# A weight product partly in float32r, and the set-up of one batch put in another order (one core)

## The chip, the core and the metric

The kernel runs on one core of a Trainium2 chip. The metric is the time of one execution on the device in microseconds (us); smaller is better. Inside the core several engines work side by side, each through its own list of instructions in a fixed order: TensorE (PE in the profile, with its weight loads shown apart as PEld), VectorE (DVE), ScalarE (ACT), GpSimd (POOL, hardly used here) and SyncE (SP, which issues DMA transfers). They wait for each other through semaphores.

## The reference

```
# attention of 512 tokens x with 32 state rows, both ways, per batch (8) and head (8), D = 64
a  = softmax(scale * x @ state^T);   xread = a  @ state
a2 = softmax(scale * state @ x^T);   sread = a2 @ x
X  = concat(xread, sread) as rows of 512        # 8 * (512 + 32) = 4352 rows
# bilinear feed-forward layer
h   = ((X @ w1) * (X @ w2)) @ w3                # w1, w2: 512 x 1024, w3: 1024 x 1024
out = h @ w_out                                 # w_out: 1024 x 512
```

The weights w1, w2, w3 and w_out come as 64-bit floats and are read as their bits; x and state come as 32-bit floats.

## The kernel before, in words

**Weights.** Each weight arrives in pieces of 128 x 1024 64-bit words (tile `raw`) and is turned into 32-bit floats by `to_f32`, in two steps: two ScalarE passes (lines 120 and 130) and then two VectorE passes, a shift (line 134) and an integer addition (line 138, a custom instruction). A caller takes the two steps one by one with `go`. There are eight pieces of w_out with half of w3, four more pieces of w3, and eight of w1 and w2 (`convert_half(n)`, n = 0 to 7). Piece n of w1 and w2 goes into `places[n]`, which is column quarter n // 2 of matrix n % 2 (0 is w1, 1 is w2) in the tile `w_sb`.

**wo = w3 @ w_out.** The reference's two last products are replaced by one with wo = w3 @ w_out, which is computed first, in eight tiles i = 0 to 7. Tile i is the sum over eight chunks k of a 128 x 128 block of w3 with `w_out[k]`, 512 columns wide, in one PSUM bank. Tiles 0 to 3 grow together while the weights arrive (`w34_first`), tiles 4 to 7 come one after the other (`w34(i)`, line 635). A float32 product stands as two records in the trace. For the chunks 4 and 6 (`SPLIT`) the first four tiles do it otherwise: each operand is split into a high part, rounded to float32r, and a low part, the remainder (`split`: a cast on ScalarE, line 99, and a subtraction on VectorE, line 100), and three float32r products (high x high, high x low, low x high; line 612) take the place of one float32 product.

`finish(i)` splits tile i of wo into its two parts, by a cast and a subtraction that read the bank. The pool `ps_o` has two banks which the tiles take in turn, so `w34(6)` needs `finish(4)` done, `w34(7)` needs `finish(5)`, and the first two accumulators of the token output (`early_stage2`) need `finish(6)` and `finish(7)`. While wo is computed, `w_out[0:8]` lies in `places[4:8]`, two chunks to a place: a conversion into place 4 + m has to wait until the last tile's product with chunks 2m and 2m + 1 has been done.

**One batch.** The scores of a batch (line 151, with x) are turned, reduced and exponentiated on VectorE and ScalarE; this gives the attention weights `at`, split into high and low. State times w1 and w2 gives the tiles `sw`, also split: for batch 0 the column half 0 is made in quarters by `sets(quarter)` (line 151 again, two products of eight pieces each, in a pool `ps_2` of three buffers), half 1 later by `sw_steps(0)[2:]`, which makes one `sw` tile from w1 (places 4 and 6) and one from w2 (places 5 and 7). `stage1(0, ft)` for ft = 0 to 7 then multiplies `sw` with `at` (line 344, 12 float32r products 128 x 512 in a block), multiplies the two results elementwise (a ScalarE copy, line 325, and a VectorE product, line 326) and splits the result into `g`. `early_stage2(quarter)` multiplies `g` with wo (line 358). So the order around the first blocks of batch 0 is: stage1 ft 0, ft 1, ft 2, the two products of half 1, `early_stage2(0)`, stage1 ft 3, and so on. After batch 0 the others follow in another form, which the change leaves alone.

**What sets the order.** TensorE and SyncE follow the order of the program. ScalarE and VectorE follow it too up to `order.close()` (line 701); behind it a scheduler sets their order by priority, and `tc.issue_after(x)` keeps the instructions in its block behind x. In either case the order is fixed when the program is built.

## Time and profile before

| | |
|---|---|
| three runs before | 488.54, 488.63, 489.65 us; median 488.63 |
| the profiled execution | 487.95 us, of which the span from the first to the last instruction is 486.2 |
| granted TensorE clock | 1.0 of full speed, over the whole span |
| busy share of the span | TensorE 99%, weight loads 76%, VectorE 81%, ScalarE 49% |
| set-up of wo and of batch 0 (up to the first stage-1 block) | 0 to 66 us |

A row of the timeline gives the start in us, the busy time in us, the engine, the line of the program, the operation, output<-input, the shape, the number of records and, in brackets, the idle time of the engine before it with what ended that. The chain of waits gives start, duration and the piece of work that ended last at that point. The changed program has other line numbers: one less between the old lines 35 and 291, and six more at the old line 635.

### The profile page before, as it was taken

What the parts mean: (1) busy time and instruction counts of PE and PEld (TensorE: products, weight loads), DVE (VectorE), ACT (ScalarE), POOL (GpSimd) and SP (SyncE); (2) the same over time, 40 slices, a digit from 0 to 9 for tenths busy, and PEclk for the clock granted to TensorE, in tenths of its full rate; (3) what the DMA queues carried; (4) which work ended last, traced back from release to release, by engine and by line L of the source; (5) the groups of instructions that cost most, each with busy time, mean ns of one, the idle gap of its engine ahead of it and who ended that gap; (6) DMA issues with size and microseconds to landing.
All of it is one profiled execution on the core that took longest, in us unless ns stands there. A gap on an engine that the chain in (4) does not pass through costs nothing.

```text
span 486.2 us, 8627 instructions
## 1 busy us (share of the span) xinstructions
PE 479.5 (99%) x3398; PEld 370.2 (76%) x3398; DVE 393.4 (81%) x580; ACT 237.6 (49%) x368; POOL 0.2 (0%) x4
## 2 busy tenths in 40 slices
PE   8999999999999999999999999999999999999996
PEld 5554467768788878887797779777977797899885
DVE  5778999798899589959985998599859985678870
ACT  4876984453547045605560555055515642353640
POOL 0000000000000000000000000000000000000000
PEclk9999999999999999999999999999999999999999
DMA  8996971163014404130413042304230223001101
GB/s 345 367 399 222 388 278 26 19 216 89 14 38 173 106 4 182 38 93 4 182 41 92 5 181 45 87 5 181 47 84 6 89 47 85 5 2 45 45 1 43
DMA packets 56361, 52.49 MB, mean 108 GB/s; under 512 B 42752, under 2 KB 50944, under 8 KB 51712
## 3 DMA queue, kind: packets, MB, share of 16 engines
q1 hardware_dynamic: 47488, 43.27, 26.8%
q10 hardware_dynamic: 8832, 8.65, 5.2%
q8 instruction: 27, 0.44, 0.4%
q14 instruction: 14, 0.11, 0.1%
HBM read 38.27 MB, written 8.91 MB: 97 GB/s over the span
## 4 chain that ended last, share of the span: by engine, by line
PE 93%; DVE 4%; ACT 1%; DMA 1%; issue 0%; DVEq 0%; ACTq 0%
PE ps L344 36%; PE ps_o L460 11%; PE ps L472 8%; PE ps L151 8%; PE ps_o L358 7%; PE ps_o L465 6%; PE ps L477 4%; PE ps L756 3%; PE ps_o L615 2%; PE ps L615 2%; PE ps_o L635 2%; PE ps L758 2%; PE ps_o L276 1%; DVE w_sb L138 1%; DMA raw<-in_w_k_dram 1%; PE ps L612 1%
## 5 line engine op out<-in xcount | busy, mean ns | idle before, releaser
L344 PE MATMUL ps<-at_lo,sw_hi 128*128 128x512 f32 x256 | 101.1, 395 | 0.0
L344 PE MATMUL ps<-at_hi,sw_hi 128*128 128x512 f32 x256 | 99.7, 389 | 0.0
L344 PE MATMUL ps<-at_hi,sw_lo 128*128 128x512 f32 x256 | 99.7, 389 | 0.0
L549 ACT COPY tmp<-ps 128x512 f32<-128x512 f32 x56 | 32.8, 585 | 121.5 <-PE ps L344 119.3
L344 PEld LDWEIGHTS ps<-at_lo,sw_hi 128*128 128x128 f32 x256 | 48.1, 188 | 15.9 <-DVE g_lo L100 4.2
L344 PEld LDWEIGHTS ps<-at_hi,sw_lo 128*128 128x128 f32 x256 | 48.1, 188 | 10.3
L344 PEld LDWEIGHTS ps<-at_hi,sw_hi 128*128 128x128 f32 x256 | 48.1, 188 | 9.5 <-issue 0.2
L488 DVE TENSOR_TENSOR tmp<-tmp,ps 128x512 f32<-128x512 f32 x42 | 28.9, 688 | 19.0 <-PE ps L477 18.1
L429 DVE TENSOR_TENSOR g_x<-tmp,ps 128x512 f32<-128x512 f32 x28 | 19.0, 679 | 26.4 <-ACT tmp L549 26.3
L100 DVE TENSOR_TENSOR sw_lo<-ps,sw_hi 128x1024 fp32r<-128x1024 f32 (+1 forms) x34 | 38.2, 1149 | 1.3 <-ACT sw_hi L99 1.3
L99 ACT CAST g_hi<-raw 128x512 fp32r<-128x512 f32 x42 | 24.6, 619 | 29.1 <-DVE raw L429 21.6
L151 PE MATMUL ps<-w_sb,st 64*32 64x512 f32 (+1 forms) x544 | 31.6, 570 | 0.4 <-DVE sw_lo L100 0.4
L99 ACT CAST sw_hi<-ps 128x1024 fp32r<-128x1024 f32 (+1 forms) x34 | 31.1, 969 | 1.8 <-PE ps L151 1.7
L460 PEld LDWEIGHTS ps_o<-t,g_hi 128*128 128x128 f32 x224 | 27.8, 191 | 5.0 <-issue 5.0
L99 ACT CAST g_hi<-g_x 128x512 fp32r<-128x512 f32 x42 | 25.6, 625 | 10.3 <-DVE g_x L429 5.3
L460 PE MATMUL ps_o<-t,g_hi 128*128 128x256 f32 x224 | 29.7, 286 | 0.0
L100 DVE TENSOR_TENSOR g_lo<-raw,g_hi 128x512 fp32r<-128x512 f32 x42 | 28.0, 681 | 1.6 <-PE ps_o L465 1.6
L460 PE MATMUL ps_o<-wo,g_hi 128*128 128x256 f32 x224 | 29.1, 283 | 0.0
L460 PEld LDWEIGHTS ps_o<-wo,g_hi 128*128 128x128 f32 x224 | 28.3, 192 | 0.5
L100 DVE TENSOR_TENSOR g_lo<-g_x,g_hi 128x512 fp32r<-128x512 f32 x42 | 27.2, 684 | 1.8 <-PE ps_o L465 1.8
L472 PE MATMUL ps<-t,g_hi 128*128 128x512 f32 x112 | 28.0, 392 | 0.0
L472 PEld LDWEIGHTS ps<-t,g_hi 128*128 128x128 f32 x112 | 20.2, 189 | 3.6
(125 smaller groups left out, 802.6 us busy)
## 6 DMA issues: line engine op xcount, KB each, us to landing
raw<-in_w_k_dram SPq DMA_DIRECT2D x8, 1024.0 KB, 6.0
x_d<-in_x_d_dram SPq DMA_DIRECT2D x8, 1024.0 KB, 7.4
raw<-in_w_dram SPq DMA_DIRECT2D x8, 1024.0 KB, 6.6
x_s<-in_x_s_dram SPq DMA_DIRECT2D x8, 1024.0 KB, 5.1
out_dram<-tmp ACTq DMA_DIRECT2D x56, 128.0 KB, 1.8
raw<-in_w3t_dram SPq DMA_DIRECT2D x4, 1024.0 KB, 7.0
e<-work SPq DMA_DIRECT2D x112, 32.0 KB, 2.0
sread<-turned SPq DMA_DIRECT2D x128, 4.0 KB, 1.7
```

Source lines behind the costliest of these rows:

```text
L99: nc.scalar.copy(out=hi, in_=src),
L100: nc.vector.tensor_tensor(out=lo, in0=src, in1=hi.bitcast(F32), op=ALU.subtract),
L151: nc.tensor.matmul(ps[j * NS:(j + 1) * NS, q], sts[b][rows, j], moving(rows, j), start=True, stop=True)
L344: nc.tensor.matmul(ps[:, i], w[:, kt, c:c + P], a[:, kt], start=(k == 0), stop=(k == 3 * KT - 1))
L358: nc.tensor.matmul(ps[:, :DO], g, wo[w][:, ft, :], start=(ft == 0 and k == 0), stop=(ft == FT - 1 and k == 2))
L460: nc.tensor.matmul(ps[:, tt * HO:(tt + 1) * HO], g, w(part, k), start=(fresh and k == 0 and tt == 0 and part == "lo"), stop=False, skip_gr ...
L465: nc.tensor.matmul(ps[:, tt * HO:(tt + 1) * HO], g, w("hi", k), start=False, stop=(k == QF - 1), skip_group_check=True)
L472: nc.tensor.matmul(ps[:, tt].rearrange("p (n d) -> p n d", n=2), g, w(k), start=(k == 0), stop=False, skip_group_check=True,)
L477: nc.tensor.matmul(ps[:, tt, :HO], g, w(k)[:, 0], start=False, stop=(k == QF - 1), skip_group_check=True)
L488: sum2 = lambda out, x, y: nc.vector.tensor_tensor(out=out, in0=x, in1=y, op=ALU.add)
L549: copied = nc.scalar.copy(out=a_sb, in_=ps[:, 0])
L615: nc.tensor.matmul(w34_ps[i][:, :DO], chunks[k][:, DO + i * P:DO + (i + 1) * P], w_out[k], start=(k == 0), stop=(k == FT - 1),)
```

## The change

There are three parts.

1. Tile 6 of wo does its chunks 4 and 6 with float32r products, as tiles 0 to 3 do. The parts of w_out that were split for those are kept and used again; the two blocks of w3 are split by a new function, `split_columns(6)`, one cast and one subtraction of 128 x 256, which stand right behind the conversion of w3's tile 6.
2. Tile 7 of wo does all its eight products before `sets(1)`, not five before and three behind. In between stand the conversions of w1's and w2's third column quarter (`convert_half(4)` and `(5)`, first steps behind the second and the fourth product; second steps ahead of and behind `sets(1)`), which a scheduler placed before.
3. `finish(6)` and `finish(7)` move out of the hand-written order, behind `convert_half(6)` and `(7)`, and behind the splits of `sets(1)`.

```
-LAST = 5
@@ sw_quarter
-        split(*(t[:, :, c * NQ:(c + 1) * NQ] for t in tiles[half, i]), ps)
+        last_split[:] = split(*(t[:, :, c * NQ:(c + 1) * NQ] for t in tiles[half, i]), ps)
@@ w34
+    spare, columns = [], {}
...
         for k in ks:
+            if (i, k) in columns:
+                hi, lo = columns[i, k]
+                w_hi, w_lo = (t[:, 0] for t in halves[k])
+                for a, b in ((hi, w_hi), (hi, w_lo), (lo, w_hi)):
+                    nc.tensor.matmul(w34_ps[i][:, :DO], a, b, start=False, stop=False)
+                continue
...
+    def split_columns(i):
+
+        both = main.tile([P, NF], F32, name="tmp", bufs=4).bitcast(F32R).rearrange("p (n k f) -> p n k f", n=2, k=len(SPLIT))
+        first, last = SPLIT
+        src = w3s[i].rearrange("p (k f) -> p k f", f=P)[:, first:last + 1:last - first]
+        split(both[:, 0], both[:, 1], src)
+        columns.update({(i, k): (both[:, 0, n], both[:, 1, n]) for n, k in enumerate(SPLIT)})
@@ the order
     go(w3_6), go(w3_6)
+    split_columns(FT - 2)
     w34(4, range(FT // 2, FT))
...
     w34(6)
     sets(0)
-    finish(6)
-    w34(7, range(LAST))
+    w1_2, w2_2 = map(convert_half, (4, 5))
+    w34(7, range(2))
+    go(w1_2)
+    w34(7, range(2, 4))
+    go(w2_2)
+    w34(7, range(4, FT))
+    go(w1_2)
     sets(1)
-    w34(7, range(LAST, FT))
-    finish(7)
+    parted = last_split[:]
+    go(w2_2)
     order.close()
...
         if quarter == 0:
-            run([partial(convert_half, n) for n in range(4, 2 * QT)])
+            with tc.issue_after(parted[0].ins), tc.issue_after(parted[1].ins):
+                run([partial(convert_half, n) for n in (6, 7)])
+                finish(6)
+                finish(7)
```

How the instructions stand now is shown at three places; what a row has is the line, the operation, output<-input by the program's names with buffer numbers, and the shape.

VectorE, from the conversion of w3's tile 6 (it lies in `sw_hi_258`) to the scores of batch 0 (`ps_2_265`). Before:

```order
L138 ISA sw_hi_258<-sw_hi_258,ulps_277 128x2048
L196 STREAM_TRANSPOSE work_287<-ps_2_265 128x1024
L199 TENSOR_REDUCE m2_288<-ps_2_265 128x2
L200 TENSOR_SCALAR m2_288<-m2_288 128x2
L218 TENSOR_REDUCE m1_291<-work_287 128x32
```

Now:

```order
L137 ISA sw_hi_258<-sw_hi_258,ulps_277 128x2048
L99 TENSOR_TENSOR tmp_283<-sw_hi_258,tmp_283 128x256
L195 STREAM_TRANSPOSE work_290<-ps_2_265 128x1024
L198 TENSOR_REDUCE m2_291<-ps_2_265 128x2
L199 TENSOR_SCALAR m2_291<-m2_291 128x2
```

The subtraction of `split_columns` stands ahead of the scores' transpose, and it reads what ScalarE casts from the conversion's output just before.

TensorE, from the two products of `sets(0)` to the first stage-1 block (`ps_o_400` before and `ps_o_405` now are tile 7 of wo). Before:

```order
L151 MATMUL ps_2_387<-w_sb_90,st_254 32x256 x8
L635 MATMUL ps_o_400<-w_sb_90,sw_lo_259 128x512 x5
L151 MATMUL ps_2_406<-w_sb_90,st_254 32x256 x8
L151 MATMUL ps_2_417<-w_sb_90,st_254 32x256 x8
L635 MATMUL ps_o_400<-w_sb_90,sw_lo_259 128x512 x3
L344 MATMUL ps_2_434<-at_lo_349,sw_hi_372 128x512
```

Now:

```order
L150 MATMUL ps_2_394<-w_sb_90,st_254 32x256 x8
L641 MATMUL ps_o_405<-w_sb_90,sw_lo_259 128x512 x8
L150 MATMUL ps_2_426<-w_sb_90,st_254 32x256 x8
L150 MATMUL ps_2_437<-w_sb_90,st_254 32x256 x8
L344 MATMUL ps_2_451<-at_lo_352,sw_hi_379 128x512
```

The eight products of the last tile stand together, and the first stage-1 block comes right behind `sets(1)`.

VectorE, from the elementwise product of stage-1 block ft 0 (into `tmp_449` before, `tmp_466` now) on. The additions of the conversions 6 and 7 read `ulps_489` and `ulps_496` before, `ulps_492` and `ulps_499` now; the products of ft 2 read `ps_2_530` before, `ps_2_537` now. Before:

```order
L326 TENSOR_TENSOR tmp_449<-tmp_449,ps_2_434 128x512
L138 ISA w_sb_90<-w_sb_90,ulps_489 128x2048
L134 TENSOR_SCALAR w_sb_90<-w_sb_90 128x1024
L100 TENSOR_TENSOR g_lo_448<-tmp_449,g_hi_447 128x512
L138 ISA w_sb_90<-w_sb_90,ulps_496 128x2048
L326 TENSOR_TENSOR tmp_469<-tmp_469,ps_2_454 128x512
L400 TENSOR_TENSOR tmp_590<-wo_93 128x512
L326 TENSOR_TENSOR tmp_545<-tmp_545,ps_2_530 128x512
L100 TENSOR_TENSOR g_lo_468<-tmp_469,g_hi_467 128x512
L261 STREAM_TRANSPOSE work_511<-e2_289 128x1024
```

Now:

```order
L326 TENSOR_TENSOR tmp_466<-tmp_466,ps_2_451 128x512
L137 ISA w_sb_90<-w_sb_90,ulps_492 128x2048
L99 TENSOR_TENSOR g_lo_465<-tmp_466,g_hi_464 128x512
L326 TENSOR_TENSOR tmp_486<-tmp_486,ps_2_471 128x512
L133 TENSOR_SCALAR w_sb_90<-w_sb_90 128x1024
L99 TENSOR_TENSOR wo_93<-ps_o_366,wo_93 128x512
L99 TENSOR_TENSOR g_lo_485<-tmp_486,g_hi_484 128x512
L326 TENSOR_TENSOR tmp_552<-tmp_552,ps_2_537 128x512
L137 ISA w_sb_90<-w_sb_90,ulps_499 128x2048
L99 TENSOR_TENSOR g_lo_551<-tmp_552,g_hi_550 128x512
L99 TENSOR_TENSOR wo_93<-ps_o_405,wo_93 128x512
L260 STREAM_TRANSPOSE work_518<-e2_292 128x1024
```

The addition of conversion 7 stood ahead of the product of ft 1 and stands behind the product of ft 2 now; the subtractions of `finish(6)` and `finish(7)` (rows that write `wo_93`) stood further up, among the splits of the sets, and stand around it now.

More of the change, by code (lines that the diff above doesn't have):

```diff
@@ L292, in attention_steps @@
         return scores, read_state, a2
+    last_split, stored = [], []
     def sw_pair():
@@ L316, in sw_quarter @@
         per_head(ps, b, lambda rows, j: w_sb[rows, quarter, i, j])
-        split(*(t[:, :, c * NQ:(c + 1) * NQ] for t in tiles[half, i]), ps)
-    last_split, stored = [], []
+        last_split[:] = split(*(t[:, :, c * NQ:(c + 1) * NQ] for t in tiles[half, i]), ps)
     def hidden(ps, n, g_hi, g_lo):
@@ L618, in w34_first @@
             )
-    spare = []
+    spare, columns = [], {}
     def convert_w3(i):
```

## The prediction, made before the changed kernel had run

> **What bounds the kernel now.** The busy shares of the profile's page come first, then TensorE's waits.
>
> ```profile
> PE 479.5 (99%) x3398; PEld 370.2 (76%) x3398; DVE 393.4 (81%) x580; ACT 237.6 (49%) x368; POOL 0.2 (0%) x4
> PE ps_o L615 <- DVE w_sb L138: 1.3, 1, 1.3
> PE ps L151 <- DVE sw_lo L100: 0.4, 1, 0.4
> ```
>
> TensorE is busy for 99% of the span, and of its waits only the last, 0.4 us, lies where the change is. Behind it TensorE never waits again. So whatever a change adds to or takes from TensorE's path before about 80 us goes to the end one for one; what happens on the other engines counts only where TensorE comes to wait. Next I read the chain of waits over the set-up of batch 0 (start, duration, piece):
>
> ```profile
> 42.58 1.45 ACT e L209 x4
> 44.03 1.05 ACT w_sb L120
> 45.08 1.07 ACT ulps L130
> ...
> 55.36 1.23 DVE sw_lo L138
> 56.59 0.60 DVE wo L100
> ...
> 62.80 0.67 PE ps L151 x16
> 63.47 2.77 PE ps_o L635 x6
> 66.24 8.20 PE ps L344 x36
> 74.44 1.88 PE ps L151 x32
> 76.32 2.94 PE ps_o L358 x12
> ```
>
> From 42.6 to 62.8 the chain runs through ScalarE and VectorE, not TensorE: there VectorE works without a pause of note, and TensorE is only just not late. How just is in the timeline:
>
> ```profile
> 38.79 1.23 DVE L138 CUSTOM_DVE_ANT_0 sw_hi<-sw_hi,ulps 128x2048 uint16<-128x2048 uint16 x1 [0.33 <-ACT ulps L130]
> 39.93 1.24 DVE L196 STREAM_TRANSPOSE work<-ps 128x1024 f32<-128x1024 f32 x1
> 42.58 0.69 ACT L209 ACTIVATE e<-ps,m 128x512 f32<-128x512 f32 x1 [3.82 <-PE ps_o L635]
> 56.50 0.68 DVE L100 TENSOR_TENSOR wo<-ps_o,wo 128x512 fp32r<-128x512 f32 x1
> 56.22 1.09 PE L151 MATMUL ps<-w_sb,st 64*32 64x256 f32 x32
> 57.25 4.56 PE L635 MATMUL ps_o<-w_sb,sw_lo 128*128 128x512 f32 x10
> 57.24 0.30 PEld L635 LDWEIGHTS ps_o<-w_sb,sw_lo 128*128 128x128 f32 x2 [0.41 <-DVE wo L100]
> 62.06 1.28 DVE L100 TENSOR_TENSOR sw_lo<-ps,sw_hi 128x512 fp32r<-128x512 f32 x2
> 62.80 0.67 PE L151 MATMUL ps<-w_sb,st 64*32 64x256 f32 x16 [0.41 <-DVE sw_lo L100]
> ```
>
> Tile 7 of wo takes the bank of tile 5, which the subtraction of `finish(5)` leaves at 56.50 + 0.68 = 57.18. Its first weight load starts at 57.24, 0.06 later. This 0.06 is also the gap between the first split of `sets(0)` (62.06 + 0.68 = 62.74) and the product that waited for it (62.80), so it is the time of a signal. Tile 7 starts when VectorE lets it, with no slack.
>
> **Part 1, the float32r columns.** Two float32 products leave TensorE and six float32r products come. The chain of waits over the whole span prices both:
>
> ```profile
> 20.34 1.72 PE ps L615 x4
> 22.06 1.38 PE ps_o L612 x6
> ```
>
> Two float32 products (four records) take 1.72, six float32r products 1.38: 0.34 less. But tile 6 ends ahead of `sets(0)`, and what follows, tile 7, waits for VectorE anyway. The gain is zero as long as VectorE is not earlier.
>
> And VectorE gets later. `split_columns` puts a cast on ScalarE (idle for 3.82 us there, row at 42.58) and a subtraction between the conversion and the scores' transpose. VectorE has to wait for the cast; the scores, ready, stand behind it. Near the end of the program there is such a round trip in just this shape:
>
> ```profile
> 469.98 0.43 DVE L763 TENSOR_TENSOR tmp<-tmp 128x256 f32<-128x256 f32 x1
> 470.44 0.41 ACT L99 CAST g_x<-tmp 128x256 fp32r<-128x256 f32 x1 [1.21 <-DVE tmp L763]
> 470.88 0.42 DVE L100 TENSOR_TENSOR g_x<-tmp,g_x 128x256 fp32r<-128x256 f32 x1 [0.47 <-ACT g_x L99]
> ```
>
> From the end of one VectorE operation (470.41) to the end of the subtraction (471.30) it is 0.89. The conversion ends at 38.79 + 1.23 = 40.02, so the subtraction ends at 40.91, and with the usual overlap of 0.08 the transpose starts at 40.83 in place of 39.93: **0.90 later**. Lower bound 0.42 (the subtraction alone, if the cast cost no wait), upper bound 1.36 (twice the 0.68 of a subtraction of double width, row at 56.50, for cast and subtraction). I take 0.90, since shape and engines are the same.
>
> The maxima behind the transpose release the exponentials at 42.58, these hold ScalarE's next conversion, and so on down the chain, which has no gap to take up 0.9. So `finish(5)` ends at 58.08 and tile 7 starts at 58.15: **+0.90**. For the same reason tile 6's own start is safe enough: it needs `finish(4)`, now 0.90 later, and a few tenths lost there vanish in the wait of tile 7.
>
> **Part 2, tile 7 whole ahead of sets(1).** From the start of tile 7 to the end of the third stage-1 block it was 57.25 to 74.44, 17.19. Now:
>
> ```profile
> 79.27 5.44 PE ps L344 x24
> 87.42 1.02 PE ps L151 x16
> 88.44 5.68 PE ps L344 x24
> ```
>
> Sixteen records of tile 7: 4.56 for ten and 6 x 0.43 = 2.58, so 7.14. Two sets: 1.03 (56.22 to 57.25). Three blocks: 8.20, plus 0.24 because they follow narrow products (5.68 against 5.44). Sum 16.61: **-0.58**. This is the old wait of 0.41 and one change fewer between kinds of products. The wait does go: the sets start at 58.15 + 7.14 = 65.3, and the splits of `sets(0)` are through by 63.34 + 0.90 = 64.2. The conversions now taken during tile 7 lie on ScalarE and VectorE beside it. The third block ends at 74.44 + 0.90 - 0.58 = 74.76, **+0.32**.
>
> **Part 3, the conversions and the low parts of wo.** No instruction is added, but the order on VectorE behind the third block matters:
>
> ```profile
> 72.66 1.22 DVE L138 CUSTOM_DVE_ANT_0 w_sb<-w_sb,ulps 128x2048 uint16<-128x2048 uint16 x1
> 74.48 0.59 ACT L325 COPY tmp<-ps 128x512 f32<-128x512 f32 x1 [1.77 <-PE ps L344]
> 75.10 0.69 DVE L326 TENSOR_TENSOR tmp<-tmp,ps 128x512 f32<-128x512 f32 x1
> 75.70 0.68 DVE L100 TENSOR_TENSOR g_lo<-tmp,g_hi 128x512 fp32r<-128x512 f32 x1
> ```
>
> Behind the third block TensorE does the two products of the column half 1 (chain: 1.88 from 74.44). The second reads w2 in places 5 and 7, so it needs the addition of conversion 7. That was done at 73.88. In the new order it stands behind the elementwise product of ft 2, which itself needs the third block and its copy. Counted from the block's end: the product starts at +0.66 (75.10 - 74.44), the addition at +1.26, it ends at +2.48, and with 0.06 TensorE starts at +2.54. It would have started at +0.94. **A new wait of 1.60**, and `early_stage2(0)`, whose operands are ready, is queued behind it. Bounds: 0 if the order did not bind, 1.60 plus whatever VectorE is late with the product of ft 2. Is it late? `sets(1)` ends at 65.3 + 1.0 = 66.3, its last cast and subtraction take about 0.6 and 0.7, so VectorE is free at 67.6. Ahead of the product of ft 2 it then has eight operations at a step of 0.60 (75.10 to 75.70) and two additions at 1.14 (1.22 less the overlap): 7.1, and some 0.4 of waits for ScalarE, 75.1. The product's copy is there at 74.76 + 0.66 = 75.4. So I add nothing.
>
> What is late next: the second accumulator needs the subtraction of `finish(7)`. On VectorE it follows the addition after 1.14 and one more subtraction (0.60): it ends at +1.26 + 1.14 + 0.60 + 0.68 = +3.68. TensorE asks for it at +2.54 + 0.94 + 0.8 (after one group of three products) = +4.3. It has 0.6 to spare. From the transpose for the state side on, VectorE is as late as TensorE is.
>
> **Sum.** +0.90 - 0.58 + 1.60 = +1.92, and 0 for the 0.34. The span goes from 486.2 to 488.1, the profiled execution from 487.95 to 489.9. The median of the runs shown lies 0.68 above that execution; put on the median, 488.63 + 1.92 is about **490.6 us**. The measurement tells about 0.3%, 1.5 us, from no change, so this is just past it.
>
> **A rule on pauses.** TensorE is to pause 1.6 us here. One pause of nearly that length is in the trace:
>
> ```profile
> PEclk9999999999999999999999999999999999999999
> 7.83 2.05 PE L615 MATMUL ps_o<-w_sb 128*128 128x512 f32 x4 [1.32 <-DVE w_sb L138]
> 9.72 1.88 PE L615 MATMUL ps<-w_sb 128*128 128x512 f32 x4
> ```
>
> After 1.32 idle the next four records took 2.05, against 1.88 without a pause, and the granted clock on the profile's page stays at 9 tenths or more throughout. The Trainium skill, "TensorE: Matmul & The Clock Gate", section "What's actually happening", says that TensorE's clock falls to half after an idle window of about 3.4 us. By that rule a pause of 1.6 costs nothing more, unless other gaps add up to a window.
>
> **The rivals.**
>
> *The detour is hidden.* If the cast is quick to start, or a gap in the chain takes up the 0.90, tile 7 starts where it did: -0.58 + 1.60 = +1.0, 489.7. For it: ScalarE is idle before the cast. Against it: the chain shows no gap, and the same-shaped trip waits 0.47.
>
> *The new wait does not come.* If conversion 7 is through in time after all (VectorE and ScalarE do keep up and the second product asks for less than I read), what is left is +0.90 - 0.58 = +0.3, 489.0.
>
> *Not slower.* Both fall away: the chain takes up the detour, the conversions keep ahead. Then TensorE gains the 0.58 and, tile 7 no longer bound, up to 0.34 more: -0.9, 487.7. It decides by whether VectorE is at tile 7 before TensorE; the 57.18 against 57.24 speaks against it.
>
> *Late twice.* VectorE is a further 1 us late at the product of ft 2, since two subtractions of 0.68 (the low parts of wo) now stand between the stage-1 operations instead of before them: the wait grows to 2.6 and the low part of `finish(7)` keeps its distance: +2.9, 491.6. For it: my margin there is 0.3 us. To this I count a fall of the clock; if the 2.94 of products behind the pause ran at half speed, 493.5.
>
> **How the numbers follow.** Forecast 0.62 (own range 490.0 to 491.2); hidden detour 0.12; no new wait 0.10; not slower 0.05; late twice 0.11. The range takes in all but the not-slower case and the far end of the last: 488.9 to 491.7. Slower by over 0.3% (490.1 or more): 0.50 of the forecast's 0.62, as its value lies only 0.5 us past the bound, and the 0.11, with 0.01 from the others: 0.62. Faster by over 0.3% (487.2 or less): 0.04, from the not-slower case. Within 0.3%: 0.34.
>
> **What would show it.** Right: TensorE waits about 1.6 us at the products of half 1 (line 150 there) for the conversion's addition (line 137); tile 7 starts near 58.15 behind the low part of wo; the wait of 0.41 at `sets(1)` is gone; VectorE idles 0.47 ahead of the new subtraction at 40 us. Wrong: tile 7 at or before 57.3, or no wait over 0.5 us between 74 and 79 us, or a new wait of TensorE behind 80 us.

## The result, and the profile of the changed kernel

The changed kernel takes 491.52 us (median of 6 runs, 490.74 to 492.88) beside 488.61 us for the kernel before on the same chip (6 runs, 488.44 to 489.83). The ratio is **1.0053, with a 95% interval of 1.0039 to 1.0067**: 2.6 us slower, from 1.9 to 3.3. (The ratio is that of the means; the medians lie 2.9 apart.) The profiled execution took 491.82 us with a span of 490.0; before it was 487.95 and 486.2. Two executions further down are left out of every ratio and median, one of the kernel before with 1233.19 us and the profiled one of the run without the columns, with 532.87 us at a granted clock of 0.851, so that no distances are given for it.

From the page of the changed kernel TensorE's granted clock, and from the view of its waits all of TensorE's waits:

```profile
PEclk9999999999999999999999999999999999999999
```

```profile
PE ps_o L641 <- DVE wo L99: 1.7, 2, 1.1
PE ps L150 <- DVE w_sb L137: 1.6, 1, 1.6
PE ps_o L77 <- DVE work L74: 1.0, 1, 1.0
PE ps_o L615 <- DVE w_sb L137: 0.8, 1, 0.8
PE ps L150 <- DVE scaled L280: 0.5, 1, 0.5
```

The columns are who waited for whom, the sum in us, how often, and the longest. The waits of the third and fourth row (lines 77 and 615) stand in the kernel before too. Three are new: for a low part of wo (1.1 us at tile 7, 0.57 at tile 6), for the addition of conversion 7 (1.6), and for `scaled`, the scaled state read-out of batch 0 (0.5). The old wait of 0.4 at `sets(1)` is gone. The clock did not fall.

The places in TensorE's timeline (start, busy time, engine and line, operation, shape, records, and the idle time before with what ended it):

```profile
50.27 3.70 PE L641 MATMUL ps_o<-w_sb,sw_hi 128*128 128x512 f32 x8 [0.57 <-DVE wo L99]
...
59.18 7.13 PE L641 MATMUL ps_o<-w_sb,sw_lo 128*128 128x512 f32 x16 [1.10 <-DVE wo L99]
...
75.66 1.09 PE L150 MATMUL ps<-w_sb,st 64*32 64x512 f32 x16
78.36 1.09 PE L150 MATMUL ps<-w_sb,st 64*32 64x512 f32 x16 [1.61 <-DVE w_sb L137]
...
103.66 1.95 PE L150 MATMUL ps<-w_sb,st 64*32 64x512 f32 x32
106.09 1.09 PE L150 MATMUL ps<-w_sb,st 64*32 64x512 f32 x16 [0.48 <-DVE scaled L280]
107.11 3.02 PE L358 MATMUL ps_o<-wo,g_x 128*128 128x512 f32 x12
```

Tile 7 starts at 59.18, before at 57.25: 1.93 later. Not all of this is the change. Higher up, ScalarE's first pass over w3's tile 6 and VectorE's addition for it stand so in the changed kernel:

```profile
37.56 1.18 ACT L119 ACTIVATE sw_hi<-raw 128x1024 f32<-128x1024 f32 x1 [0.91 <-DMA raw<-in_w3t_dram]
...
39.83 1.22 DVE L137 CUSTOM_DVE_ANT_0 sw_hi<-sw_hi,ulps 128x2048 uint16<-128x2048 uint16 x1 [0.36 <-ACT ulps L129]
41.52 0.42 DVE L99 TENSOR_TENSOR tmp<-sw_hi,tmp 128x256 fp32r<-128x256 f32 x1 [0.47 <-ACT tmp L98]
41.87 1.24 DVE L195 STREAM_TRANSPOSE work<-ps 128x1024 f32<-128x1024 f32 x1
```

The weights of that tile landed late in this execution: ScalarE waited 0.91 us for the transfer, and the addition starts at 39.83, against 38.79 in the profile of the kernel before. Nothing that the change touches lies ahead of it (the transfers up to there are issued in the same order), and over the other profiles of this study the same ScalarE wait is between 0 and 1.5 us. So 1.04 of the 1.93 is how one execution differs from another. To take this out, distances below count **from the start of this addition** ("the mark"). Tile 7 started 18.46 behind the mark before (57.25 - 38.79) and 19.35 now: +0.89. The products of stage 2 with ft 6 (line 358, `g_x`), which are the last of the part that the change moves, started 64.47 behind it before (103.26) and 67.28 now (107.11): **+2.81**. That is the change's cost by the traces, within the 1.9 to 3.3 that the times give. These are TensorE's rows of before:

```profile
100.53 2.81 PE L151 MATMUL ps<-w_sb,st 64*32 64x512 f32 x48
103.26 3.04 PE L358 MATMUL ps_o<-wo,g_x 128*128 128x512 f32 x12
```

From there to the end of the span it is 382.9 us before (486.2 - 103.26) and 382.9 now (490.0 - 107.11), so nothing behind this point adds to the cost.

The 2.81 come to pieces like this, all from rows above, the rows of before that the prediction shows, and the chains of waits: +0.89 up to tile 7; from tile 7 to the end of the third block 16.57 now (59.18 to 75.75, where the block ends in the chain of waits) and 17.19 before, -0.62; the two products of half 1 up to the first product of stage 2 take 3.7 (75.7 to 79.4) in place of 1.9, +1.8, of which 1.61 is the wait; and from the sets at 103.66 to the products at 107.11 it is 3.45 where the kernel before took 2.73 (100.53 to 103.26), +0.72, of which 0.48 is the wait. At both waits about **0.24 us more** is lost than the wait itself.

### The profile page after: what moved, and what is told of

It is laid out like the page before. It is cut to its first block, busy times and chain, and to the rows that moved or that the text cites. A ratio compares the mean times of both kernels' runs of the same rounds, so it can differ in the third digit from the quotient of the medians.

```text
span 490.0 us, 8633 instructions
## 1 busy us (share of the span) xinstructions
PE 480.5 (98%) x3400; PEld 371.1 (76%) x3400; DVE 394.0 (80%) x581; ACT 238.2 (49%) x369; POOL 0.2 (0%) x4
## 4 chain that ended last, share of the span: by engine, by line
PE 84%; DVE 6%; DMA 6%; ACT 3%; issue 0%; ACTq 0%; DVEq 0%; SPq 0%
PE ps L344 35%; PE ps_o L460 11%; PE ps L472 8%; PE ps L150 7%; PE ps_o L358 6%; PE ps_o L465 5%; PE ps L477 4%; DMA raw<-in_w_k_dram 4%; PE ps L779 3%; DMA raw<-in_w3t_dram 2%; PE ps L781 2%; PE ps_o L275 1%; PE ps_o L641 1%; ACT ulps L129 1%; DVE w_sb L137 1%; ACT w_sb L119 1%
```

## The experiments

Each was timed five times or more against the kernel before on the same chip, and profiled once. Part 1 alone to subtraction late shared 30 runs of the kernel before (median 489.47 us); maxima first, three undone, tile 7 released and the one without the columns 24 (488.59); scaled first, products later and bound lifted 25 (489.10); and the last 17 (489.66). "Tile 7" and "ft 6" are distances from the mark, in us, as defined above.

| kernel | ratio to before, 95% | tile 7 | ft 6 | ft 6 against before |
|---|---|---|---|---|
| before | 1 | 18.46 | 64.47 | |
| changed | 1.0053 (1.0039 to 1.0067) | 19.35 | 67.28 | +2.81 |
| part 1 alone | 1.0019 (1.0009 to 1.0028) | 19.33 | 65.87 | +1.40 |
| parts 2 and 3 alone | 0.9999 (0.9987 to 1.0010) | 18.44 | 65.04 | +0.57 |
| conversion first | 1.0010 (0.9999 to 1.0021) | 19.33 | 65.19 | +0.72 |
| subtraction late | 1.0032 (1.0016 to 1.0047) | 18.45 | 66.59 | +2.12 |
| maxima first | 1.0058 (1.0045 to 1.0071) | 19.34 | 67.32 | +2.85 |
| three undone | 1.0021 (1.0009 to 1.0034) | 18.46 | 65.04 | +0.57 |
| tile 7 released | 1.0022 (1.0012 to 1.0031) | 17.53 | 65.38 | +0.91 |
| ... without the columns | 1.0036 (1.0024 to 1.0049) | | | |
| scaled first | 1.0035 (1.0023 to 1.0048) | 19.33 | 66.65 | +2.18 |
| products later | 1.0014 (1.0003 to 1.0025) | 19.34 | 66.12 | +1.65 |
| bound lifted | 1.0003 (0.9992 to 1.0014) | 17.30 | 65.02 | +0.55 |
| conversions sooner | 0.9997 (0.9985 to 1.0008) | 17.34 | 63.92 | -0.55, but +1.03 behind 125 us |

One per mille is 0.49 us. The distances agree with the timed ratios to about 0.6 us, which is the half-width of the intervals, but for two rows: products later has +1.65 beside a time of +0.7, and the last one has a wait behind the point where the table ends. In every row with distances but the last the way from ft 6 to the end of the span is 382.8 to 383.1 us, so the distance holds what the change costs in that execution; in the last it is 384.7.

**Part 1 alone** (the float32r columns with `split_columns`; the order of before for all else).

> The kernel before with part 1 alone: tile 6 of wo does chunks 4 and 6 in float32r, everything else stands as before. Theory (the detour): the subtraction of the w3 columns holds VectorE's chain up by 0.90 us at 41 us, tile 7 of wo starts that much later, and the 0.34 us that TensorE saves go into its wait: +0.9 us, 489.5 (+0.2%). VectorE shows an idle time of about 0.47 ahead of the 128x256 subtraction and TensorE a wait of about 1.1 at tile 7 for the low part of wo. Rival (all of the loss is in the conversions' order): VectorE has slack for the detour and TensorE gains its 0.34: -0.3 us, 488.3, and no wait over 0.2 at tile 7.

The place of the detour in VectorE's timeline:

```profile
39.94 1.23 DVE L138 CUSTOM_DVE_ANT_0 sw_hi<-sw_hi,ulps 128x2048 uint16<-128x2048 uint16 x1 [0.36 <-ACT ulps L130]
41.64 0.42 DVE L100 TENSOR_TENSOR tmp<-sw_hi,tmp 128x256 fp32r<-128x256 f32 x1 [0.47 <-ACT tmp L99]
41.98 1.24 DVE L196 STREAM_TRANSPOSE work<-ps 128x1024 f32<-128x1024 f32 x1
```

The detour is there in full: the transpose starts 2.04 behind the mark in place of 1.14 (39.93 - 38.79), and tile 7 is 0.87 later. The six float32r products gain nothing: TensorE waits 1.08 us at tile 7 for the low part of wo. The time, +0.19% or 0.9 us, is what was expected. The trace shows 1.40 up to ft 6, since in this build VectorE's order near 97 us also differs and the low part of ft 5 comes late, which holds up stage 2 by about 0.4 (3.15 us up to the next block, 99.14 - 95.99, in place of 2.72).

**Parts 2 and 3 alone**: the changed kernel without its `split_columns`.

```
-    split_columns(FT - 2)
```

> The changed kernel without part 1: tile 6 of wo in float32 throughout, tile 7 whole ahead of sets(1), its conversions and low parts of wo as changed. The order on VectorE that comes out has the addition of conversion 7 ahead of the product of ft 2 and not behind it. Theory: no detour, so tile 7 starts at 57.2; the third stage-1 block ends 0.6 earlier than before; the wait for conversion 7 is small (0 to 0.5); the late wait for the read state near 105 us (0.5 and about 0.2 of broken stream) stays: -0.6 to +0.6 us, 488.0 to 489.2, most likely 488.7. Rival (the new place of tile 7 and of the low parts costs by itself, whatever conversion 7 does): +1.9 us or more, 490.5.

No change of time. Tile 7 is where it was (18.44), the third block ends 0.67 earlier by the mark, and the wait for conversion 7 hardly comes, because in this build the addition slipped ahead of the product of ft 2. TensorE waits 0.26 there (the view puts it down to the copy of ft 2, but that copy and the addition, which by the program the product needs, both end at 76.06) and 0.48 at `scaled`; each again loses some 0.24 more. So the sum of the two experiments is not the whole: the wait of 1.6 stands and falls with VectorE's order, and that order comes out differently when something far ahead of it is changed.

**Conversion 7 first**: the changed kernel with the addition of conversion 7 put back ahead of the product of ft 1.

```
-        stage1(0, 2 * quarter + 1, gs)
+        if quarter == 0:
+            with tc.issue_after(parted[0].ins), tc.issue_after(parted[1].ins):
+                run([partial(convert_half, n) for n in (6, 7)])
+        with tc.issue_after(added[0].ins) if quarter == 0 else ExitStack():
             stage1(0, 2 * quarter + 1, gs)
...
-                run([partial(convert_half, n) for n in (6, 7)])
```

(`added` holds the last integer addition of `to_f32`.)

> The changed kernel with one more order on VectorE: the product of ft 1 stands behind the addition of conversion 7 (so that of ft 2 does too). Nothing is added or taken away. Theory: the wait of 1.6 at the second product of half 1 goes or falls under 0.4, the detour of 0.9 stays: 1.3 to 1.8 us faster than the changed kernel, 1.1 to 1.6 slower than before, 490.0. Rival (VectorE is simply behind, and any order makes TensorE wait for something): the wait moves to the accumulators or to the first g, and the time stays within 0.5 us of the changed kernel, 491.3.

```profile
75.83 1.09 PE L151 MATMUL ps<-w_sb,st 64*32 64x512 f32 x16 [0.24 <-DVE tmp L327]
```

The wait of 1.61 is down to 0.24, now for a bank that the product of ft 1 frees, and the time falls from +0.53% to +0.10%. The wait at `scaled` went as well, though nothing was done for it; why shows further down. Of the 2.09 us that ft 6 gains by the mark, 1.37 come at the two products of half 1, which lose 0.48 here (2.35 us in place of 1.87) and 1.85 in the changed kernel, and 0.72 at `scaled`. So the order of these two pieces on VectorE is the largest cost of the change. What is left is the detour (tile 7 at 19.33) and this 0.48, less the gain at tile 7.

**Subtraction late**: the changed kernel with `split_columns` cut in two, the cast where it was and the subtraction behind softmax's first subtraction. There the cast has long been done, and VectorE idled for ScalarE's conversion in any case (0.24 and 0.56 us in the kernel before, at 45.11 and 46.36).

```
-        split(both[:, 0], both[:, 1], src)
+        nc.scalar.copy(out=both[:, 0], in_=src)
...
     go(softmax), go(softmax), go(softmax)
+    subtract_columns()
     go(w1_0), go(softmax), go(w1_0)
```

> The changed kernel with the subtraction of the w3 columns moved behind the scores' maxima and the first subtraction of the softmax, ahead of the shift of the conversion, where VectorE idled 0.24 and 0.56 us for ScalarE. Theory: the detour is hidden entirely, tile 7 starts 0.9 earlier, everything else stands: 0.9 us faster than the changed kernel, 2.0 slower than before, 490.6. Rival (the detour is harmless, the profile's late start was only the transfer of the weights): same as the changed kernel, 491.5.

Tile 7 is at 18.45 again: the detour costs nothing there once VectorE needn't wait and the exponentials aren't held up. The wait for conversion 7 is 1.83 here, 0.2 longer, since VectorE comes to the product of ft 2 about 0.2 late, and the late wait stays at 0.48, so of the 0.9 at tile 7 some 0.7 reach ft 6.

**Maxima first**: the changed kernel with the score maxima of batch 1 ahead of the product of ft 5 on VectorE. There the changed kernel has this order (rows of VectorE, changed kernel):

```profile
95.20 0.69 DVE L326 TENSOR_TENSOR tmp<-tmp,ps 128x512 f32<-128x512 f32 x1 [0.72 <-ACT tmp L325]
95.80 1.22 DVE L198 TENSOR_REDUCE m<-ps 128x2 f32<-128x1024 f32 x1
...
103.42 0.68 DVE L326 TENSOR_TENSOR tmp<-tmp,ps 128x512 f32<-128x512 f32 x1
104.02 1.22 DVE L246 TENSOR_TENSOR work<-work,sum 128x1024 f32<-128x1024 f32 x1
105.15 0.68 DVE L99 TENSOR_TENSOR g_x<-tmp,g_x 128x512 fp32r<-128x512 f32 x1
105.75 0.28 DVE L280 TENSOR_TENSOR scaled<-ps,sum 128x128 f32<-128x128 f32 x1
```

VectorE idles 0.72 ahead of the product of ft 5, because it stands ahead of the maxima (line 198), which were ready. That looked like the cause of the wait at `scaled`.

```
-        stage1(0, 2 * quarter + 1, gs)
+        with tc.issue_after(maxed[0].ins) if quarter == 2 else ExitStack():
+            stage1(0, 2 * quarter + 1, gs)
```

(`maxed` holds the reduction of line 198.)

> The changed kernel, with one order on VectorE put back: the score maxima of batch 1 ahead of the elementwise product of ft 5, as the kernel before has it. Theory (the late wait near 106 us comes from that swap, since VectorE idles 0.72 us ahead of the product there): the wait of 0.48 for the scaled state goes, the 0.24 of a broken stream with it, the group of 48 products behind it starts 69.6 us after the start of the addition for w3 tile 6 (70.4 in the changed kernel, 67.6 in the one before), and the time is 0.7 us under the changed kernel's, a ratio of about 1.0038. Rival (VectorE is late there anyway, because the scores' state blocks came late by transfer, and the order does not matter): the wait stays between 0.3 and 0.5, ratio 1.005. The wait of 1.6 at conversion 7 stays in both.

```profile
102.86 0.69 DVE L326 TENSOR_TENSOR tmp<-tmp,ps 128x512 f32<-128x512 f32 x1 [0.40 <-ACT tmp L325]
103.46 1.22 DVE L246 TENSOR_TENSOR work<-work,sum 128x1024 f32<-128x1024 f32 x1
104.59 0.68 DVE L99 TENSOR_TENSOR g_x<-tmp,g_x 128x512 fp32r<-128x512 f32 x1
105.20 0.28 DVE L280 TENSOR_TENSOR scaled<-ps,sum 128x128 f32<-128x128 f32 x1
```

The theory fell. The idle time of 0.72 is gone, 0.40 of it came back at the product of ft 7, and the wait is 0.48 as before; the time did not move. The order of the kernel before shows what is different here:

```profile
99.16 1.22 DVE L247 TENSOR_TENSOR work<-work,sum 128x1024 f32<-128x1024 f32 x1
100.30 0.68 DVE L326 TENSOR_TENSOR tmp<-tmp,ps 128x512 f32<-128x512 f32 x1
100.90 0.28 DVE L281 TENSOR_TENSOR scaled<-ps,sum 128x128 f32<-128x128 f32 x1
102.26 0.65 DVE L100 TENSOR_TENSOR g_x<-tmp,g_x 128x512 fp32r<-128x512 f32 x1
```

In the kernel before `scaled` follows the product of ft 7 directly, 0.60 us behind it. In the changed kernel and in this one two operations stand in between: the multiplication of the softmax (`work<-work,sum`, 1.13 up to the next start) and the subtraction for ft 7 (`g_x`, 0.60). So `scaled` starts 2.33 and 2.34 behind the product. In the conversion-first kernel `scaled` stands ahead of both. That gave the next experiment.

**Scaled first**: the changed kernel with that subtraction behind `scaled`, nothing else of its own (the split of ft 7 is written behind `scaled`, the read-out's first step on VectorE, and held behind it by `issue_after`).

> The changed kernel with the last subtraction of stage 1 (the low part of ft 7, 0.6 us) behind the scaling of the state read-out on VectorE instead of ahead of it; nothing else of its own. Theory (the late wait near 106 us comes from this place in VectorE's order: in the traces so far the four kernels with the subtraction ahead wait 0.5 there, the others do not): the wait of 0.48 goes and the 0.24 of a broken stream with it, the group of products behind it starts 69.6 us after the addition for w3 tile 6 in place of 70.4, ratio 1.0038. Rival (VectorE is more than 0.5 us late there, from the wait for the moved blocks): a wait of 0.1 to 0.3 stays, ratio 1.005.

```profile
104.04 0.28 DVE L280 TENSOR_TENSOR scaled<-ps,sum 128x128 f32<-128x128 f32 x1
104.24 0.68 DVE L99 TENSOR_TENSOR g_x<-tmp,g_x 128x512 fp32r<-128x512 f32 x1
...
102.55 2.92 PE L150 MATMUL ps<-w_sb,st 64*32 64x512 f32 x48
105.40 3.02 PE L361 MATMUL ps_o<-wo,g_x 128*128 128x512 f32 x12
```

The 48 records run through without a wait, and ft 6 comes 0.63 earlier by the mark. The idle time ahead of the product of ft 5 is still there (0.97 in this execution) and costs nothing. So moving one of the two operations away, 0.6 us, is enough to take the late wait away; moving the multiplication alone was not tried. The four kernels with the subtraction ahead of `scaled` (the changed one, parts 2 and 3 alone, subtraction late, maxima first) wait about 0.5 there; the others don't.

**Three undone**: subtraction late, conversion 7 first and maxima first at once.

> The changed kernel with its three measured costs undone at once: the subtraction of the w3 columns behind softmax's first subtraction, conversion 7 ahead of the product of ft 1, batch 1's maxima ahead of the product of ft 5. Theory (the three costs are separate and add up): nothing of the detour, -0.6 from tile 7 whole, 0.3 of wait and 0.2 of a broken stream at conversion 7, no late wait: the group of 48 products starts 67.5 us after the addition for w3 tile 6, as in the kernel before within 0.3, ratio 1.000 (0.999 to 1.001). Rival (something else in the change costs time, which the named costs hid): 68.3 or more, ratio 1.002.

The three waits are gone (0.26 is left at the second product of half 1), the third block ends 0.64 before that of the kernel before by the mark, and still the time is 0.2% above it. In this build the scheduler has put the low part of ft 5 behind the product of ft 6, and stage 2 waits for it. The third edit alone did not do that (in maxima first the low part stands ahead of that product), so it comes from the edits together:

```profile
95.99 0.69 DVE L327 TENSOR_TENSOR tmp<-tmp,ps 128x512 f32<-128x512 f32 x1
96.60 0.69 DVE L99 TENSOR_TENSOR g_lo<-tmp,g_hi 128x512 fp32r<-128x512 f32 x1
...
96.53 0.73 PE L359 MATMUL ps_o<-wo,g_hi 128*128 128x512 f32 x2
97.34 0.50 PE L359 MATMUL ps_o<-wo,g_lo 128*128 128x512 f32 x1
```

The low part is done at 97.29 and the product that needs it starts at 97.34, 0.35 later than its neighbours' step of 0.46 would have it. Up to the next block stage 2 takes 3.20 us here in place of 2.72. By the table +0.57 is left; the time says 1.0 with an interval of 0.4 to 1.7.

**Tile 7 released**: the same, and VectorE's transpose of the token weights (1.16 us) behind the low part of tile 5; then the same **without the columns** (tile 6 all in float32).

```
-    go(w3_7), go(w1_1), go(softmax), go(w3_7)
+    go(w3_7), go(w1_1), go(w3_7)
     finish(5)
     go(softmax)
     go(w1_1)
+    go(softmax)
```

> The kernel of the run before it in this list, and VectorE's transpose of the token weights (1.16 us) behind the low part of tile 5 instead of ahead of it, so that tile 7 of wo is no longer bound by VectorE. Theory (the 0.34 us that the six float32r products save on TensorE was swallowed by VectorE's lateness at tile 7, and comes out once that is gone): tile 7 starts without a wait, 18.0 us after the addition for w3 tile 6 in place of 18.45, and the group of 48 products at 67.1; ratio 0.999. Rival (the delayed transpose makes the next operand late, and the gain goes into a wait between the sets and the first stage-1 block): a wait of 0.3 to 1.2 there, ratio 1.000 to 1.002.

> The kernel of the run before it in this list without part 1: tile 6 takes all its products in float32. Theory (with tile 7 released, the six float32r products are worth 0.34 us): tile 6 takes 0.34 longer on TensorE and the time is 0.34 us above that of the run before, ratio 0.9997. Rival (the saving is swallowed by another wait): the same time within 0.1 us. The order on VectorE behind the sets may differ from that run, which would show as a wait at conversion 7.

```profile
57.01 7.13 PE L642 MATMUL ps_o<-w_sb,sw_lo 128*128 128x512 f32 x16
...
76.13 1.09 PE L151 MATMUL ps<-w_sb,st 64*32 64x512 f32 x16 [1.52 <-DVE tmp L327]
```

Tile 7 no longer waits, and by the mark it starts 0.93 earlier than in the kernel before. (Where tile 7 doesn't wait for VectorE, how much this is depends on how late the weights landed, so the distance holds for the execution shown.) All of it is lost again 16 us later: the second product of half 1 waits 1.52 us, for a bank that the product of ft 1 frees, which stands behind conversion 7. The rival was right in kind, but it put the wait in the wrong place. Without the columns the median was 490.43 (6 runs) against 489.90 us, and the ratios' intervals overlap (1.0024 to 1.0049 and 1.0012 to 1.0031). That points the way the theory said, but it doesn't settle what the six products are worth in the time. On TensorE alone the traces do: tile 6 takes 6.63 us with them (49.35 to 55.98 in the tile 7 released kernel) and 6.96 without (49.26 to 56.22 in the kernel before), both without a wait, so 0.33.

**Products later**: the changed kernel with TensorE's order changed. Early stage 2 of ft 0 and 1 follows the third block, and the two products of half 1 stand behind stage 1 of ft 3; on VectorE the conversions 6 and 7 are behind the low part of ft 1.

```
+        if quarter == 2:
+            early_stage2(1)
         stage1(0, 2 * quarter, gs)
-        if quarter == 1:
-            run(sw_steps(0)[2:])
-        if quarter:
+        if quarter in (1, 3):
             early_stage2(quarter - 1)
...
         stage1(0, 2 * quarter + 1, gs)
         if quarter == 1:
+            run(sw_steps(0)[2:])
```

> The changed kernel with TensorE's order changed: the two products of column half 1, which need conversion 7, stand behind stage 1 of ft 3 instead of ahead of early stage 2, the first early stage 2 (products with ft 0 and 1) directly behind the third block, and conversions 6 and 7 on VectorE behind the low part of ft 1. Theory (the wait of 1.6 is there only because these products follow the third block at once): no wait for the conversion at all, the detour of 0.9 and the -0.6 of tile 7 stay, no wait at the scaled state: the products with ft 6 of stage 2 start 64.8 to 65.0 us after the addition for w3 tile 6 (67.3 in the changed kernel, 64.5 in the one before), ratio 1.0008. Rival (the wait moves on: the split of half 1 is now late for stage 1 of ft 4): a wait of 0.5 to 1.5 at that stage, ratio 1.002 to 1.004.

```profile
PE ps L150 <- DVE w_sb L137: 0.6, 1, 0.6
PE ps_o L358 <- DVE g_lo L99: 0.2, 1, 0.2
```

Neither theory was right in full. The wait doesn't vanish behind 5.5 us of cover, it shrinks to 0.6, and 0.2 come at a low part. The 0.2 costs more than its length: stage 2 of ft 2 and 3 takes 3.36 us up to the next block, in place of 2.85 for such a group in the kernel before (76.25 to 79.10). The time falls to +0.14%.

**Bound lifted**: this with the subtraction late and the transpose behind tile 5. **Conversions sooner**: this again, with conversions 6 and 7 bound to VectorE's order alone, so that ScalarE may start them earlier, and the sums of parts of wo (line 400) behind the split of half 1.

> The kernel of the run before it in this list, with the subtraction of the w3 columns behind softmax's first subtraction and the transpose of the token weights behind the low part of tile 5. Theory (VectorE's lateness was what swallowed the saving on TensorE; with tile 7 free and no wait behind it the saving goes through to the end): tile 7 starts 17.5 us after the addition for w3 tile 6 (18.45 before), the third block ends at 34.0 (35.6 before), the products with ft 6 of stage 2 start at 62.9 to 63.2 (64.5 before), ratio 0.9972. Rival (VectorE becomes the bound in stage 1, and TensorE waits for a low part): waits of 1 us or more between 74 and 95 us, ratio 0.9995 to 1.001.

> The bound-lifted kernel with conversions 6 and 7 bound to VectorE's order alone, so that ScalarE starts them in its idle time ahead of the third block, and the two sums of parts of wo behind the split of half 1 in place of ahead of conversion 7. Theory (what the bound-lifted kernel lost again was the wait of 1.6 for conversion 7, which came late because of 1.2 us of sums on VectorE and of ScalarE's late start): the wait shrinks to 0.5 or less, the products with ft 6 of stage 2 start 63.2 to 63.8 us after the addition for w3 tile 6 (64.5 before, 65.0 in the bound-lifted kernel), ratio 0.998. Rival (VectorE as a whole is full in this stage, so what is put off comes back): waits of 1 us or more at the scaled state near 102 us or at the low parts of stage 1, ratio 0.9995 to 1.0015.

The bound-lifted kernel ends its third block 1.85 us earlier by the mark (33.74 against 35.59) and loses it again: a wait of 1.57 at the second product of half 1, and a small one at a low part. So the rival had the time right and the theory had not. The last kernel takes this wait away, gets one of 0.49 for the cast of ft 0 at the first stage 2 (ScalarE takes the conversions ahead of it), and TensorE is 0.55 ahead of the kernel before at ft 6. Then this happens, in its timelines of VectorE, of the DMA queue and of TensorE:

```profile
111.54 1.24 DVE L260 STREAM_TRANSPOSE work<-e 128x1024 f32<-128x1024 f32 x1
112.84 11.85 SPq L174 DMA_DIRECT2D e<-work  x16
126.10 1.05 PE L275 MATMUL ps_o<-x_s,e 128*32 128x64 f32 x58 [1.32 <-DMA e<-work]
```

And in the kernel before:

```profile
108.41 1.24 DVE L261 STREAM_TRANSPOSE work<-e 128x1024 f32<-128x1024 f32 x1
109.72 12.19 SPq L175 DMA_DIRECT2D e<-work  x16
123.91 1.10 PE L276 MATMUL ps_o<-x_s,e 128*32 128x64 f32 x64
```

The state read-out of batch 1 needs sixteen transfers that follow a VectorE transpose. In the last kernel the queue is through at 124.69 and TensorE goes on at 126.10, 1.41 later. With the same 1.41 the kernel before has its blocks at 121.91 + 1.41 = 123.3 and asks for them at 123.9: it has about 0.6 us to spare (an estimate from these rows). VectorE, with all that was put off, is 2.0 us later at this transpose by the mark (71.63 against 69.62). So in this execution the gain on TensorE is given back 20 us further down: the product behind the read-out starts 87.18 behind the mark (127.09), before 86.15 (124.94), +1.03. The twelve timed runs allow at most +0.4, so how much a usual execution gives back is not shown. That is nearer to the rival, which looked for such a wait at another place. Neither kernel's time can be told from that of the kernel before: no version here beats it.

## Why the prediction was right, and where it was not

**The number.** The median of 491.52 lies in the stated range (488.9 to 491.7), but not in the forecast's own (490.0 to 491.2). It is nearer to the 491.6 of the late-twice rival than to the forecast's 490.6, and yet that rival did not come about. The costs that were forecast came nearly as forecast; that two more, set at nothing, still left the time in the range was luck.

**The detour, +0.90.** Right to 0.01: tile 7 is +0.89 by the mark (part 1 alone +0.87), VectorE idles 0.47 ahead of the subtraction as in the like-shaped trip near the end of the program, and subtraction late makes it vanish. The hidden-detour rival is out. The prediction also had tile 6 right: it waits 0.57 for `finish(4)`, and this vanishes in the wait of tile 7. One reading was not exact: VectorE does not work "without a pause of note" from 42.6 on, it idles 0.24 and 0.56 for ScalarE. The pauses hang on the same chain, so they did not take up the detour, but they are the place where subtraction late hides its work.

**The 0.34 of TensorE.** Right in size (0.33 by tile 6 itself) and right that it is swallowed at tile 7. That it would come out once VectorE is earlier was not shown: each kernel that freed tile 7 met the next wait on VectorE.

**Tile 7 whole, -0.58.** Measured -0.62 in the changed kernel, -0.65 in parts 2 and 3 alone (16.48 us from tile 7 to the products of half 1, 74.86 - 58.38, before 17.13). The wait of 0.41 went as said.

**The new wait, 1.60.** Measured 1.61, for conversion 7's addition, at the forecast place. These are VectorE's rows behind the third block, whose end at 75.75 releases ScalarE's copy:

```profile
76.39 0.69 DVE L326 TENSOR_TENSOR tmp<-tmp,ps 128x512 f32<-128x512 f32 x1
77.00 1.22 DVE L137 CUSTOM_DVE_ANT_0 w_sb<-w_sb,ulps 128x2048 uint16<-128x2048 uint16 x1
78.13 0.68 DVE L99 TENSOR_TENSOR g_lo<-tmp,g_hi 128x512 fp32r<-128x512 f32 x1
78.73 0.68 DVE L99 TENSOR_TENSOR wo<-ps_o,wo 128x512 fp32r<-128x512 f32 x1
```

The product was forecast 0.66 behind the block's end and is at +0.64, the addition at +1.26 and is at +1.25. The late-twice rival did not come about, but its margin was 0.14 and not 0.3 (VectorE could have started at 76.23, one step of 0.60 behind 75.63; the copy was through at 76.37), and subtraction late overran it. `finish(7)` is through at 79.41, 3.66 behind the block's end (forecast 3.68), and TensorE does not wait for it. The 1.60 was meant as the difference of two starts (+2.54 and +0.94), and the 1.61 is idle time. As a difference of starts it is 1.67: TensorE starts at 78.36, +2.61, which is 0.14 behind the end of the addition (78.22) and not 0.06. The second product then takes longer too, and the products of half 1 lose 1.82 in all. So the term was too small by 0.22, what an interrupted stream costs beside the idle time. The prediction had a cost of this size in its rows (5.68 against 5.44 us for blocks behind narrow products) and used it for the blocks, not for the wait.

**The step that failed** is the last sentence of part 3: "From the transpose for the state side on, VectorE is as late as TensorE is." It holds for the transpose itself (79.33 against 76.31, +3.02, with TensorE +3.13 at the first product of stage 2). Further on, VectorE's order was not the old one. The product of ft 7 is still only as late as TensorE (103.42 against 100.30, +3.12). `scaled` is at 105.75 against 100.90, +4.85, behind the multiplication (1.13) and the subtraction (0.60) that used to stand elsewhere; that is 1.73 more, and TensorE had some 1.25 of room there (the 1.73 less the wait). It cost 0.48 + 0.24. The prediction's own list named "a new wait of TensorE behind 80 us" as a sign that it is wrong, and it came. The order of the instructions is fixed when the program is built, so it could be read beforehand that `scaled` had changed places; the orders shown ahead of the prediction end at the transpose.

**The sum.** +0.89 - 0.62 + 1.8 + 0.72 = 2.8 by the trace and 2.6 by the times, against a forecast of +1.92; the 0.9 between the traces and the forecast is 0.22 at the wait and 0.72 at `scaled`, less 0.05 from the other two terms. The forecast for the profiled execution, 489.9, was missed by 1.9: 0.9 by these terms and 1.0 by the weights that landed later.

**The rule on pauses.** TensorE paused 1.61 us. The twelve products of stage 2 that followed took 2.95 (79.45 to 82.40 in the chain of waits), against 2.94 before, and the granted clock stayed at 9 tenths or more in every slice of the page. The Trainium skill, "TensorE: Matmul & The Clock Gate", section "What's actually happening", puts the idle window at about 3.4 us. The traces agree as far as they go: the pauses of 1.61 us here and of 1.83 in subtraction late left the clock at 9 tenths or more, and no trace here tests one as long as the window. The Trainium skill, "TensorE: Matmul & The Clock Gate", section "Single matmul latency", gives a lone bf16 product about 0.17 us of latency on top of its streaming time; as an estimate by that section an interruption would cost about this much once. The rows here say 0.24.

## What to carry to other kernels

A saving on the engine that is 99% busy is worth nothing at a point where another engine only just keeps up; look for the rows in which its start follows someone else's end by 0.06 us, and ask how late that engine gets when more work stands ahead of it. An order that a scheduler makes must be compared to the end of the stage, not only around the edit: here two operations of 1.7 us together came to stand ahead of a third, 30 us behind the edit, and cost as much as the edit's own gain. And where several waits on one engine are undone one after the other, expect the next one: before freeing a stage, look up the slack of the transfers that follow from it.

## What was unexpected

The landing of one weight tile, early in the program, moves the whole execution: ScalarE's wait for it is 0 in the profile of the kernel before and from 0 to 1.5 us in the others, and the runs of the kernel before in the experiments lie mostly between 487.7 and 490.7 us. A span of one execution against another cannot show a change of 1 us; distances from a mark inside the program can, as long as the engine at the mark is the one that sets the start of what follows.

An interrupted stream of like products costs 0.24 us beyond the wait, whatever its length: between the two products of half 1 with waits of 0.24, 0.26, 0.60, 1.57 and 1.61 us (conversion first, parts 2 and 3 alone, products later, bound lifted, changed), the way from the first of them to the next kind of product is longer than the 1.87 of before by 0.48, 0.50, 0.85, 1.81 and 1.85. In the changed kernel 0.15 of the 0.24 comes from how the profile counts: it ends the first product 1.09 us after its start, while in the unbroken stream the next one starts after 0.94. The other 0.09 is in the second product (78.36 to 79.38, 1.02 in place of 0.94).
